# K and V rows of half the heads swapped by halves, scores by quadrants in one visit, intra products in two halves

## The chip, the cores and the metric

The kernel runs on one core of a Trainium2 chip. The metric is the device time of one execution, in microseconds (us); smaller is better. Before the change it is 224.65 us, the median of 8 runs (224.59 to 225.79).

## What is computed

The reference is a linear attention with decay over 4 batch rows, 8 heads, 768 positions and head dimension 64, followed by a gated layer on all 3072 tokens:

```python
for b in range(nb):
    ...
    intra = np.einsum('bhic,bhjc->bhij', qb, kb) * Dmask[None]
    intra = np.einsum('bhij,bhjd->bhid', intra, vb)
    inter = np.einsum('bhid,bhde->bhie', qb * lam_pow[None], kv_state)
    out[:, :, sl] = intra + inter
    ...
    kv_state = lam_block[None, :, None, None] * kv_state + np.einsum('bhsd,bhse->bhde', kb_dec, vb)
...
gate = 1.0 / (1.0 + np.exp(-(x @ w_gate)))
val = x @ w_val
return (gate * val @ w_out).astype(np.float32)
```

`Dmask` is zero where a key comes after its query (`rel < 0`), and `lam` to the power of their distance elsewhere. The result does not depend on the block length: the reference uses 64 positions, the kernel 128.

## The kernel before, in words

The 768 positions are 6 blocks (`NSTEP`) of 128 (`C`), numbered 0 to 5. One block holds 4 images (batch rows, `B`) of 8 heads, so 512 tokens. For each block the kernel runs attention and then the gated layer: `gv` computes the 12 hidden tiles (for each, four matmuls with WG, L432, a sigmoid on ScalarE, L435, four matmuls with WV, L438, a product on VectorE, L441), and `piece_po` the 12 matmuls of one output tile of 128 tokens (L495), its copy (L498) and its store (L503). The order of the work on every engine is written out by hand: each engine executes its instructions in the order of the program, and the attention of block n+1 is written in between the gated layer of block n (lines 691 to 722).

In blocks 2 to 5, which the change touches, the attention has these steps.

- **Loads** (`load`, L70): GpSimd issues DMAs that read q, k and v from HBM as float32 and write bf16. q and k are split by even and odd heads into two DMAs each (L77); v is one DMA (L91). They are issued one block ahead, behind `fade` (L394) and `make_kd` (L385), which also run on GpSimd.
- **Transposes** (`transpose_by_dma`, L229): two DMAs issued by SyncE turn q and k into QR and KR, with 64 head dimensions of two heads on the 128 partitions. `u` is the half of the partitions that a head lies on. `scale` (L242, VectorE) multiplies QR by the powers of lam and gives QS.
- **Scores** (`piece_s`, L299): for each image and head, keys by queries, 128 x 128, over 64 dimensions. `most_scores` takes images 0 to 2, with a weight tile of 64 rows and 128 columns; two heads, one on each half of the rows, run beside each other. `last_scores` takes image 3 in `parts=2`, as pieces of 64 keys, four beside each other. One PSUM bank (`sp`) holds four heads of one image. Of the four 64 x 64 quadrants of a head's scores, the one with late keys and early queries is masked to zero afterwards.
- **Masks** (`piece_m`, L204): VectorE multiplies a bank by the mask and writes bf16, 8 banks in a block.
- **Inter** (`piece_x`, L326): state Sb by QS, 32 matmuls of 64 x 64 weights and 128 queries, into four banks `op`.
- **Intra** (`add_intra` and `piece_a`, both through `intra`, L312): V of a head (128 keys by 64) by its masked scores, 128 queries, added into the same `op`; 32 in a block, two beside each other.
- **take_xt** (L343): ScalarE copies `op` to XT, the input of the gated layer. **c** (L416): the update of the state from kd and V, 32 matmuls of 64 columns, and its sum into Sb on VectorE (L423); block 5 has none.

The scores of images 0 to 2 stand between `gv(n, 10)` and `gv(n, 11)`, and the rest (`visit`) between the second and third `piece_po`. In block 5 `last_scores` stands there, and `piece_a` behind the third. Block 2 has its attention between the output tiles of blocks 0 and 1 (lines 678 to 690). PSUM has 8 banks: 5 in the pool `ps` and 3 in the pool `ff`, through which the gated layer rotates.

Of the kernel before, what the change touches and what calls it, by code (L numbers as in the profile page):

```python
# [15 lines left out]
def kernel(  # L16
# [14 lines left out]
    C = 128  # L31
# [35 lines left out]

    Q, K, V = {}, {}, {}

    def load(n, what, b0, b1):  # L70
        sl = slice(n * C, (n + 1) * C)
        for c in what:
            lst, src = {"q": (Q, q), "k": (K, k), "v": (V, v)}[c]
            if n > 1 and c != "v":
                lst[n] = qkv.tile([128, 2, B, HP, D], BF16, tag=c + "b", name=c + "b")
                for e in range(2):
                    nc.gpsimd.dma_start(  # L77
                        out=lst[n][:, e].rearrange("p b y d -> p (b y) d"),
                        in_=src[:, e::2, sl, :].rearrange("b y s d -> s (b y) d"))
# [11 lines left out]
            nc.gpsimd.dma_start(  # L91
                out=lst[n][:, b0:b1],
                in_=src[b0:b1, :, sl, :].rearrange("b h s d -> s (b h) d"))
# [77 lines left out]
    for u in range(2):  # L171
        us = slice(u * 64, (u + 1) * 64)
        nc.scalar.activation(dec[us, :].rearrange("p (e x) -> p e x", e=2),
                             lnl[us, :].rearrange("p (x u e) -> p u e x", u=2, e=2)[:, u],
                             AF.Exp, scale=float(C))
    lamq = const.tile([128, HP, C], BF16, tag="lamq")
    mask = const.tile([128, H, C], FP32, tag="mask")

    lp = const.tile([128, HP, C], FP32, tag="lp")

    def lamq_start():
        for u in range(2):
# [9 lines left out]
    def lamq_end():  # L192
        nc.vector.tensor_copy(lamq, lp)
# [6 lines left out]
    def masked(out, x, n, u):  # L200
        if n == 0:
# [6 lines left out]
    def half(e):  # L208
        return slice(e * 64, (e + 1) * 64)

    def head(g, u):
        return 4 * (g % 2) + 2 * u + g // 2
# [76 lines left out]
    def piece_s(n, bs, homes=("ps", "ps"), parts=1):  # L289
        w = C // parts  # L290
        for b in bs:
            bp, i = b // 2, b % 2
            sp = [psum_at(homes[u]) for u in range(2)]
            for hp in range(HP):
                for u in range(2):
                    us = slice(u * 64, (u + 1) * 64)
                    for z in range(parts):
                        zs = slice(z * w, (z + 1) * w)
                        nc.tensor.matmul(sp[u][zs, hp, :], lhsT=KS[n, bp][us, hp // 2, i, hp % 2, zs],  # L299
                                         rhs=QS[n, bp][us, hp // 2, i, hp % 2, :],  # L300
                                         start=(hp == 0), stop=(hp == HP - 1), skip_group_check=True)
            SP[n, b] = sp

    def piece_m(n, b, us=(0, 1)):
        if (n, b) not in MT:
            MT[n, b] = mtp.tile([128, 2, HP, C], BF16, tag="MT", name="MT")
        for u in us:
            masked(MT[n, b][:, u], SP[n, b][u], n, u)

    def intra(n, b, out, m, start, stop):  # L310
        for e in range(2):
            nc.tensor.matmul(out[half(e)], lhsT=V[n][:, b, 2 * m + e, :],  # L312
                             rhs=MT[n, b][:, e, m, :] if n == 0 else MT[n, b][:, m % 2, 2 * e + m // 2, :],
                             start=start, stop=stop, skip_group_check=True)
# [3 lines left out]
    def piece_x(n, bp, homes=("ps", "ps")):  # L318
# [3 lines left out]
        for i in range(2):  # L322
            for x in range(2):
                for u in range(2):
                    for e in range(2):
# [6 lines left out]
    def add_intra(n, b, first=True):  # L332
        bp, i = b // 2, b % 2
        for u in range(2):
            for x in range(2):
                intra(n, b, OP[bp, u][:, x, i, :], 2 * x + u, False, not first and x == 1)
# [36 lines left out]
    def make_kd(n):  # L373
        if n == 1:
            KD[n] = kdp.tile([128, 2, B * H * D // 2], BF16, tag="kd", name="kd")
            for bp in range(NB2):
                ko, ki = (x[n][:, bp].rearrange("p (e b y d) -> p e b y d", e=2, b=2, y=HP) for x in (KD, K))
                for e in range(2):
                    nc.gpsimd.tensor_tensor(
                        out=ko[:, e], in0=ki[:, e],  # L380
                        in1=kds[:, e::2].unsqueeze(1).unsqueeze(3).to_broadcast([128, 2, HP, D]), op=ALU.mult)
            return
        KD[n] = kdp.tile([128, 2, B, HP, D], BF16, tag="kd", name="kd")
        for e in range(2):
            nc.gpsimd.tensor_tensor(  # L385
                out=KD[n][:, e], in0=K[n][:, e],
                in1=kds[:, e::2].unsqueeze(1).unsqueeze(3).to_broadcast([128, B, HP, D]), op=ALU.mult)

    SD = {}

# [119 lines left out]

    idle(10)
    nc.vector.tensor_copy(Q[0][:, 0], q01[0])
    piece_tq0([0])
    make_mask(0)
    make_mask(1)
# [46 lines left out]
    def t(n, bp):  # L562
        piece_t(n, bp)

    def most_scores(n):
        piece_s(n, [0, 1])
        piece_s(n, [2], ("ps", "ff"))
        piece_m(n, 2, (1,))

    def other_masks(n):  # L570
        piece_m(n, 0)
        piece_m(n, 1)
        piece_m(n, 2, (0,))

    def last_scores(n):
        piece_s(n, [3], parts=2)
        piece_m(n, 3)
        piece_x(n, 0)
        piece_x(n, 1, ("ps", "ff"))

    def visit(n):
        last_scores(n)
        for i in range(2):
            add_intra(n, i, i == 0)
        take_xt(n, 0)
        add_intra(n, 2)
        c(n, 0, 1, homes=("ps", "ff"))
        add_intra(n, 3, False)
        take_xt(n, 1)

    def pair(bp):
        piece_s(1, [2 * bp], ("ff", "ps"), parts=2)
# [43 lines left out]
        load_wo(i, NFT // 3)  # L636
    gv(0, 6)
    lamq_end()
    gv(0, 7)
    gv(0, 8)  # L640
    g9 = psum()
# [33 lines left out]
    make_kd(2)  # L675
    load(3, "qkv", 0, B)
    gvh(1, 1, *range(NFT))
    piece_po(0, 0)
    piece_po(0, 1)
    piece_po(0, 2)  # L680
    t(2, 0)
    t(2, 1)
    piece_po(0, 3)
    most_scores(2)
    other_masks(2)
    piece_po(1, 0)
    piece_po(1, 1)
    visit(2)
    piece_po(1, 2)
    piece_po(1, 3)  # L690
    for n in range(2, NSTEP):
        nx = n + 1
        if nx == NSTEP:
            gv(n, *range(NFT))
            for tt in range(B - 1):
                piece_po(n, tt)
            piece_last(n, B - 1)
            break
        transpose_by_dma(nx)
        gv(n, 0, 1)  # L700
        if nx + 1 < NSTEP:
            fade()
            make_kd(nx)
            load(nx + 1, "qkv", 0, B)
        gv(n, 2, 3, 4, 5, 6, 7, 8)
        t(nx, 0)
        gv(n, 9)
        t(nx, 1)
        gv(n, 10)
        most_scores(nx)  # L710
        gv(n, 11)
        other_masks(nx)
        piece_po(n, 0)
        piece_po(n, 1)
# [38 lines left out]
```

## Time and profile before

| | |
|---|---|
| time, median of 8 runs | 224.65 us |
| the profiled execution, its time | 224.72 us |
| its span, first to last instruction | 222.9 us |
| granted TensorE clock | 1.00 |
| L204, a mask of one bank (128x512) on VectorE | 683 ns, 40 in blocks 1 to 5 |
| L242, the scaling of half a block's QR | 685 ns |
| L77, issue of a DMA of q or k on GpSimd | 1183 and 1178 ns |
| L385, half of kd on GpSimd | 1908 ns |
| L343, copy of one bank to XT on ScalarE | 599 ns |

The profile is one execution. Its busy times are per engine; a wait is charged to what released it. The weight load of a matmul is a row of its own (PEld). The duration of a matmul in these rows, some 200 to 400 ns, is its whole passage through the array; matmuls overlap, so what one costs is the distance of its start from the next start. Tile sizes in front of a matmul's shape, such as 64*128, are the rows and columns of the array that it uses.

### The profile page before, as it was taken

To read this page: it belongs to the slowest core of one execution; us is meant where nothing else is said; L and a number is where in the kernel's file an instruction comes from. 1 tells how busy PE (TensorE), PEld (TensorE's weight loads), DVE (VectorE), ACT (ScalarE), POOL (GpSimd) and SP (SyncE) were. 2 spreads that over 40 slices of the span, in tenths; PEclk is the share of its full clock that TensorE was granted. 3 is DMA by queue.
4 is the path that set the end of the run, shared out by engine and by line. 5 is a ranking of instruction groups with operands and counts; after the bars stand their busy time and mean duration, and the time that the engine had idled before them with its cause. 6 is when DMAs were issued, how large, how long until landed. Compare 5 with 4: busy or idle time off the path is not lost.

```text
span 222.9 us, 4362 instructions
## 1 busy us (share of the span) xinstructions
PE 214.9 (96%) x1786; PEld 114.2 (51%) x1808; DVE 106.6 (48%) x193; ACT 79.3 (36%) x151; POOL 79.2 (36%) x78
## 2 busy tenths in 40 slices
PE   7689999999999999999999999999999999999994
PEld 2444455888854564444464444564444445444443
DVE  7797658596412641346740435760335750333300
ACT  5664333435412243333243333152333225333221
POOL 8997698993593049700029900000000000000000
PEclk9999999999999999999999999999999999999999
DMA  6999999999999992999722999721900021100022
GB/s 109 156 168 193 192 176 156 156 195 172 157 141 177 241 218 100 120 151 156 48 97 85 129 149 156 48 97 49 235 0 0 3 93 51 47 0 0 3 94 96
DMA packets 106420, 25.72 MB, mean 115 GB/s; under 512 B 97056, under 2 KB 103456, under 8 KB 106400
## 3 DMA queue, kind: packets, MB, share of 16 engines
q0 software_dynamic: 81792, 13.90, 82.3%
q1 hardware_dynamic: 23568, 11.28, 23.8%
q10 hardware_dynamic: 1040, 0.26, 0.5%
q8 instruction: 14, 0.23, 0.4%
q14 instruction: 6, 0.05, 0.1%
HBM read 28.32 MB, written 6.29 MB: 155 GB/s over the span
## 4 chain that ended last, share of the span: by engine, by line
PE 92%; DMA 3%; POOL 3%; issue 1%; ACT 0%; DVE 0%; POOLq 0%
PE po L495 27%; PE vp L438 20%; PE gp L432 20%; PE gp L446 6%; PE gp L467 5%; PE vp L473 5%; DMA vb<-in_v_dram 3%; PE op L312 3%; PE sp L299 3%; PE po L484 1%; POOL kb L91 1%; PE cp L416 1%; PE op L326 1%; POOL qb L91 1%; POOL vb L91 1%
## 5 line engine op out<-in xcount | busy, mean ns | idle before, releaser
L441 DVE TENSOR_TENSOR ht<-sg,vp 128x512 bf16<-128x512 bf16 x52 | 35.7, 687 | 70.4 <-PE vp L438 69.3
L495 PE MATMUL po<-WO,ht 128*128 128x512 bf16 x266 | 60.9, 379 | 0.6
L438 PE MATMUL vp<-XT,WV 128*128 128x512 bf16 x203 | 52.9, 379 | 0.4
L432 PE MATMUL gp<-XT,WG 128*128 128x512 bf16 x204 | 52.5, 379 | 0.2 <-issue 0.2
L435 ACT ACTIVATE sg<-gp 128x512 bf16<-128x512 f32 x52 | 31.0, 597 | 59.9 <-PE gp L432 56.5
L495 PEld LDWEIGHTS <-ht 128*128 128x128 bf16 x276 | 26.5, 98 | 31.5
L438 PEld LDWEIGHTS <-WV 128*128 128x128 bf16 x208 | 20.3, 98 | 24.6
L432 PEld LDWEIGHTS <-WG 128*128 128x128 bf16 x208 | 20.0, 98 | 24.0
L498 ACT COPY ob<-po 128x512 f32<-128x512 f32 x23 | 13.5, 586 | 50.3 <-PE po L495 48.5
L204 DVE TENSOR_TENSOR MT<-sp,mask 128x512 bf16<-128x512 f32 x40 | 25.2, 683 | 11.3 <-PE sp L299 11.3
L394 POOL TENSOR_TENSOR sd<-Sb,dec 128x512 f32<-128x512 bf16 x8 | 8.1, 1038 | 35.5 <-DVE Sb L423 35.4
L467 PE MATMUL gp<-XT,WG 128*128 128x256 bf16 x96 | 14.4, 273 | 0.0
L473 PE MATMUL vp<-XT,WV 128*128 128x256 bf16 x96 | 14.4, 273 | 0.0
L477 DVE TENSOR_TENSOR ht<-sg,vp 128x256 bf16<-128x256 bf16 x24 | 10.0, 420 | 8.4 <-PE vp L473 8.4
L470 ACT ACTIVATE sg<-gp 128x256 bf16<-128x256 f32 x24 | 9.2, 385 | 12.7 <-PE gp L467 12.7
L91 POOL DMA_DIRECT2D vb<-in_v_dram x10 | 12.7, 1278 | 2.4 <-issue 1.8
L385 POOL TENSOR_TENSOR kd<-kb,kds 128x1024 bf16<-128x1024 bf16 x6 | 11.3, 1908 | 5.0 <-PE gp L467 5.0
L343 ACT CAST XT<-op 128x512 bf16<-128x512 f32 x19 | 9.9, 599 | 2.4 <-PE op L312 2.4
L473 PEld LDWEIGHTS <-WV 128*128 128x128 bf16 x96 | 9.4, 98 | 1.1
L467 PEld LDWEIGHTS <-WG 128*128 128x128 bf16 x96 | 9.2, 98 | 1.4
L77 POOL DMA_DIRECT2D qb<-in_q_dram x8 | 9.4, 1183 | 0.0
L77 POOL DMA_DIRECT2D kb<-in_k_dram x8 | 9.3, 1178 | 0.0
(82 smaller groups left out, 165.4 us busy)
## 6 DMA issues: line engine op xcount, KB each, us to landing
out_dram<-ob SPq DMA_DIRECT2D x21, 256.0 KB, 2.0
kb<-in_k_dram POOLq DMA_DIRECT2D x10, 256.0 KB, 12.8
qb<-in_q_dram POOLq DMA_DIRECT2D x8, 256.0 KB, 10.1
vb<-in_v_dram POOLq DMA_DIRECT2D x4, 512.0 KB, 16.5
WO<-in_moe_w_out_dram POOLq DMA_DIRECT2D x3, 512.0 KB, 8.1
WV<-in_moe_w_val_dram POOLq DMA_DIRECT2D x5, 256.0 KB, 8.9
WG<-in_moe_w_gate_dram POOLq DMA_DIRECT2D x4, 256.0 KB, 8.5
qb<-in_q_dram POOLq DMA_DIRECT2D x6, 128.0 KB, 8.5
```

The costliest lines, as they stand in the source:

```text
L77: nc.gpsimd.dma_start(out=lst[n][:, e].rearrange("p b y d -> p (b y) d"), in_=src[:, e::2, sl, :].rearrange("b y s d -> s (b y) d"))
L91: nc.gpsimd.dma_start(out=lst[n][:, b0:b1], in_=src[b0:b1, :, sl, :].rearrange("b h s d -> s (b h) d"))
L204: nc.vector.tensor_tensor(out=out.rearrange("p (e x) c -> p e x c", e=2), in0=x.rearrange("p (e x) c -> p e x c", e=2), in1=mask.rearrange ...
L432: nc.tensor.matmul(gp, lhsT=WG[:, mt, fs], rhs=x[:, mt, :], start=(mt == 0), stop=(mt == NMT - 1))
L435: nc.scalar.activation(sg, gp, AF.Sigmoid)
L438: nc.tensor.matmul(vp, lhsT=WV[:, mt, fs], rhs=x[:, mt, :], start=(mt == 0), stop=(mt == NMT - 1))
L441: nc.vector.tensor_mul(HT[n, ft], sg, vp)
L446: nc.tensor.matmul(ps[:, lo:hi], lhsT=W[:, mt, ft * 128:(ft + 1) * 128], rhs=x[:, mt, lo:hi], start=(mt == 0), stop=(mt == NMT - 1))
L467: nc.tensor.matmul(gp[:, cs], lhsT=WG[:, mt, fs], rhs=x[:, mt, cs], start=(mt == 0), stop=(mt == NMT - 1))
L473: nc.tensor.matmul(vp[:, cs], lhsT=WV[:, mt, fs], rhs=x[:, mt, cs], start=(mt == 0), stop=(mt == NMT - 1))
L495: nc.tensor.matmul(po, lhsT=HT[n, ft][:, tt * 128:(tt + 1) * 128], rhs=WO[:, ft, :], start=(ft == 0), stop=(ft == NFT - 1))
L498: nc.scalar.copy(ob, po)
```

## The change

K and V of blocks 2 to 5 are loaded so that heads 1, 2, 5 and 6 have their two halves of 64 rows (positions) swapped: `turned` issues, for K and for V, two DMAs for heads in order and four for the swapped ones, each on 64 partitions. Tables for swapped rows are made once (`other_halves`, `half_tables`, `make_mask3`), and `make_kd` uses such a table. The scores of all four images are computed in one visit (`all_scores`), 64 keys at a time: where keys are the early half, against all 128 queries, and where they are the late half, against the late 64 queries only. The remaining three quadrants of a head are packed into 6 banks instead of 8 (`slot`), and 6 masks take the place of 8. The intra product is done in two halves: for early queries over 64 keys (`intra_low`), for late queries over 128 keys (`intra_high`). A drain of TensorE stands between the inter products and `intra_low`. In block 2 the scores and the visit each stand one output tile later than before; in blocks 3 to 5 all scores stand where `most_scores` stood, and in block 5 the whole visit where `last_scores` stood.

```diff
+    def turned(src, n, dst):
+        for r in (0, 3, 1, 2):
+            halves = [(slice(0, 128), 0, C)] if r in (0, 3) else [(half(z), (1 - z) * 64, 64) for z in range(2)]
+            for rows, lo, k in halves:
+                nc.gpsimd.dma_start(
+                    out=dst(rows, r).rearrange("p b y d -> p (b y) d"),
+                    in_=src[:, r::4, n * C + lo:n * C + lo + k, :].rearrange("b y s d -> s (b y) d"))
...
-            if n > 1 and c != "v":
+            if n > 1 and c == "k":
+                lst[n] = qkv.tile([128, 2, B, HP, D], BF16, tag=c + "b", name=c + "b")
+                turned(src, n, lambda rows, r: lst[n][rows, r % 2, :, r // 2::2, :])
+                continue
+            if n > 1 and c == "v":
+                lst[n] = qkv.tile([128, B, H, D], BF16, tag=c + "b", name=c + "b")
+                turned(src, n, lambda rows, r: lst[n][rows, :, r::4, :])
+                continue
+            if n > 1:
...
+    def other_halves():
+        for z, d in ((0, -64.0), (1, 64.0)):
+            nc.vector.tensor_scalar_add(jns[half(z)], jn[half(z)], d)
+        for t, i in ((pks, 0), (kd4, 1)):
+            nc.scalar.activation(t, lnl, AF.Exp, scale=jns[:, i:i + 1])
+
+    def half_tables():
+        for z, d in ((0, 64.0), (1, -64.0)):
+            nc.vector.tensor_scalar_add(p1s[half(z)], p1[half(z)], d)
+        nc.vector.tensor_scalar(out=tris, in0=ip1, scalar1=p1s, scalar2=None, op0=ALU.is_ge)
+        nc.vector.tensor_copy(kds2, kds)
+        nc.vector.tensor_copy(kds2.rearrange("p (x r) -> p x r", r=4)[:, :, 1:3],
+                              kd4.rearrange("p (x r) -> p x r", r=4)[:, :, 1:3])
...
+    def make_mask3():
+        m3 = mask3.rearrange("p u t (s c) -> p u t s c", c=64)
+        def put(out, rows, cols, u, e):
...
+            nc.vector.tensor_tensor(
+                out=out, in0=t[rows, cols].unsqueeze(1).unsqueeze(1).to_broadcast([k, 3, 2, 64]),
+                in1=p[rows, 2 * u + e::4].unsqueeze(1).unsqueeze(3).to_broadcast([k, 3, 2, 64]), op=ALU.mult)
+        for u in range(2):
+            for e in range(2):
+                put(m3[:, u, :, 1 + e:5 + e:3, :], slice(0, 128), slice(64, 128), u, e)
+            for z in range(2):
+                put(m3[half(z), u, :, 0:4:3, :], half(z), slice(0, 64), u, u ^ z)
+        for t, f in ((0, slice(0, 2)), (1, slice(2, 6, 3)), (2, slice(3, 5))):
+            nc.vector.tensor_copy(m3[:, :, t, 6:8, :], m3[:, :, 0, f, :])
...
-    lp = const.tile([128, HP, C], FP32, tag="lp")
+    lp = mask3[:, 0, 0, :].rearrange("p (h c) -> p h c", h=HP)
...
+    def slot(b, x, k):
+        return (b, 3 * x + k) if b < 3 else (1, 6 + x) if k == 2 else (2 * x, 6 + k)
...
+    def all_scores(n):
+        for t in range(3):
+            for u in range(2):
+                ST[t, u] = granules(psum_at("ff" if t == 2 and u else "ps").rearrange("p h c -> p (h c)"))
+            MU[n, t] = mtp.tile([128, 2, TCH], BF16, tag="MT", name="MT")
+        for b in range(B):
+            bp, i = b // 2, b % 2
+            for x in range(2):
+                for low in (True, False):
+                    for e in range(2):
+                        for u in range(2):
+                            z = half(u ^ e if low else 1 - (u ^ e))
+                            w = KS[n, bp][half(u), e, i, x, z]
+                            r = QS[n, bp][half(u), e, i, x, :].rearrange("p (k c) -> p k c", c=64)
+                            (t, s0), (t1, s1) = slot(b, x, 0), slot(b, x, 1 + e)
+                            if low and t == t1:
+                                nc.tensor.matmul(ST[t, u][z, s0:s1 + 1:s1 - s0, :], lhsT=w, rhs=r,
+                                                 start=(b < 3 and x == 0), stop=False, skip_group_check=True)
+                                continue
+                            if low:
+                                nc.tensor.matmul(ST[t, u][z, s0, :], lhsT=w, rhs=r[:, 0, :],
+                                                 start=False, stop=False, skip_group_check=True)
+                            nc.tensor.matmul(ST[t1, u][z, s1, :], lhsT=w, rhs=r[:, 1, :],
+                                             start=False, stop=False, skip_group_check=True)
+
+    def all_masks(n, *which):
+        for t, u in which:
+            nc.vector.tensor_tensor(out=granules(MU[n, t][:, u, :]), in0=ST[t, u],
+                                    in1=granules(mask3[:, u, t, :]), op=ALU.mult)
+
+    def intra_low(n, b, x, e):
...
+        for u in range(2):
+            rows = half(u ^ e)
+            nc.tensor.matmul(OP[bp, u][half(e), x, i, 0:64], lhsT=V[n][rows, b, 4 * x + 2 * u + e, :],
+                             rhs=MU[n, t][rows, u, s0 * 64:(s0 + 1) * 64], ...
+
+    def intra_high(n, b):
...
+        for u in range(2):
+            for x in range(2):
+                for e in range(2):
+                    t, s0 = slot(b, x, 1 + e)
+                    nc.tensor.matmul(OP[bp, u][half(e), x, i, 64:128],
+                                     lhsT=V[n][:, b, 4 * x + 2 * u + e, :],
+                                     rhs=MU[n, t][:, u, s0 * 64:(s0 + 1) * 64], ...
...
-                in1=kds[:, e::2].unsqueeze(1).unsqueeze(3).to_broadcast([128, B, HP, D]), op=ALU.mult)
+                in1=kds2[:, e::2].unsqueeze(1).unsqueeze(3).to_broadcast([128, B, HP, D]), op=ALU.mult)
...
     def visit(n):
-        last_scores(n)
-        for i in range(2):
-            add_intra(n, i, i == 0)
-        take_xt(n, 0)
-        add_intra(n, 2)
-        c(n, 0, 1, homes=("ps", "ff"))
-        add_intra(n, 3, False)
-        take_xt(n, 1)
+        for bp in range(NB2):
+            piece_x(n, bp)
+        nc.tensor.drain()
+        for e in range(2):
+            for i in range(2):
+                for x in range(2):
+                    intra_low(n, i, x, 1 - e)
+                    intra_low(n, 2 + i, x, e)
+        for bp in range(NB2):
+            for i in range(2):
+                intra_high(n, 2 * bp + i)
+            take_xt(n, bp)
+        if n + 1 < NSTEP:
+            c(n, 0, 1, homes=("ps", "ff"))
...
     piece_po(0, 3)
-    most_scores(2)
-    other_masks(2)
     piece_po(1, 0)
+    all_scores(2)
+    all_masks(2, (2, 1), (0, 0), (0, 1), (1, 0), (1, 1), (2, 0))
     piece_po(1, 1)
+    piece_po(1, 2)
     visit(2)
-    piece_po(1, 2)
     piece_po(1, 3)
...
-        most_scores(nx)
+        all_scores(nx)
+        all_masks(nx, (2, 1))
         gv(n, 11)
-        other_masks(nx)
+        all_masks(nx, (0, 0), (0, 1), (1, 0), (1, 1), (2, 0))
         piece_po(n, 0)
         piece_po(n, 1)
-        if nx + 1 < NSTEP:
-            visit(nx)
-            piece_po(n, 2)
-        else:
-            last_scores(nx)
-            piece_po(n, 2)
-            piece_a(nx, 0, 1)
+        visit(nx)
+        piece_po(n, 2)
         piece_po(n, 3)
```

Left out of the diff are the declarations of the new tables and the places of three calls: `other_halves()` behind the copy of q at L512, `half_tables()` behind `lamq_end()` at L638, and `make_mask3()` in front of `piece_po(0, 0)` at L678.

More of the change, by code (lines that the diff above doesn't have):

```diff
@@ L68, with half @@
     Q, K, V = {}, {}, {}
+    def half(e):
+        return slice(e * 64, (e + 1) * 64)
+    def turned(src, n, dst):
[5 more added lines that the diff above has]
+                    in_=src[:, r::4, n * C + lo:n * C + lo + k, :].rearrange("b y s d -> s (b y) d"))
     def load(n, what, b0, b1):
@@ L175, with granules @@
                              AF.Exp, scale=float(C))
+    jns = const.tile([128, 2], FP32, tag="jns")
+    pks = const.tile([128, H], FP32, tag="pks")
+    kd4 = const.tile([128, H], FP32, tag="kd4")
+    kds2 = const.tile([128, H], FP32, tag="kds2")
+    tris = const.tile([128, C], FP32, tag="tris")
+    p1s = const.tile([128, 1], FP32, tag="p1s")
+    mask3 = const.tile([128, 2, 3, TCH], FP32, tag="mask3")
+    def other_halves():
[10 more added lines that the diff above has]
+                              kd4.rearrange("p (x r) -> p x r", r=4)[:, :, 1:3])
+    def granules(t):
+        return t.rearrange("p (s c) -> p s c", c=64)
+    def make_mask3():
+        m3 = mask3.rearrange("p u t (s c) -> p u t s c", c=64)
+        def put(out, rows, cols, u, e):
+            t, p = (tris, pks) if u ^ e else (tri, pk)
+            k = rows.stop - rows.start
+            nc.vector.tensor_tensor(
[8 more added lines that the diff above has]
+            nc.vector.tensor_copy(m3[:, :, t, 6:8, :], m3[:, :, 0, f, :])
     lamq = const.tile([128, HP, C], BF16, tag="lamq")
     mask = const.tile([128, H, C], FP32, tag="mask")
-    lp = const.tile([128, HP, C], FP32, tag="lp")
+    lp = mask3[:, 0, 0, :].rearrange("p (h c) -> p h c", h=HP)
     def lamq_start():
@@ L206, in masked @@
             in1=mask.rearrange("p (x u e) c -> p u e x c", u=2, e=2)[:, u], op=ALU.mult)
-    def half(e):
-        return slice(e * 64, (e + 1) * 64)
     def head(g, u):
@@ L302, in piece_s @@
             SP[n, b] = sp
+    def slot(b, x, k):
+        return (b, 3 * x + k) if b < 3 else (1, 6 + x) if k == 2 else (2 * x, 6 + k)
+    ST, MU = {}, {}
+    def all_scores(n):
[22 more added lines that the diff above has]
+                                             start=False, stop=False, skip_group_check=True)
@@ new lines, in all_masks @@
+    def all_masks(n, *which):
[3 more added lines that the diff above has]
+    def intra_low(n, b, x, e):
+        bp, i = b // 2, b % 2
+        t, s0 = slot(b, x, 0)
+        for u in range(2):
+            rows = half(u ^ e)
+            nc.tensor.matmul(OP[bp, u][half(e), x, i, 0:64], lhsT=V[n][rows, b, 4 * x + 2 * u + e, :],
+                             rhs=MU[n, t][rows, u, s0 * 64:(s0 + 1) * 64],
+                             start=False, stop=False, skip_group_check=True)
@@ new lines, in intra_high @@
+    def intra_high(n, b):
+        bp, i = b // 2, b % 2
+        for u in range(2):
[4 more added lines that the diff above has]
+                                     lhsT=V[n][:, b, 4 * x + 2 * u + e, :],
+                                     rhs=MU[n, t][:, u, s0 * 64:(s0 + 1) * 64],
+                                     start=False, stop=False, skip_group_check=True)
@@ L330, in piece_x @@
                                          skip_group_check=True)
[L332 to L336, printed above, removed]
     def take_xt(n, bp):
@@ L512 @@
     nc.vector.tensor_copy(Q[0][:, 0], q01[0])
+    other_halves()
     piece_tq0([0])
@@ L563, in t @@
         piece_t(n, bp)
[L565 to L579, printed above, removed]
-    def visit(n):
-        last_scores(n)
-        for i in range(2):
-            add_intra(n, i, i == 0)
-        take_xt(n, 0)
-        add_intra(n, 2)
-        c(n, 0, 1, homes=("ps", "ff"))
-        add_intra(n, 3, False)
-        take_xt(n, 1)
+    def visit(n):
+        for bp in range(NB2):
[12 more added lines that the diff above has]
+            c(n, 0, 1, homes=("ps", "ff"))
     def pair(bp):
@@ L638 @@
     lamq_end()
+    half_tables()
     gv(0, 7)
@@ L677 @@
     gvh(1, 1, *range(NFT))
+    make_mask3()
     piece_po(0, 0)
```

## Prediction

> **What bounds the kernel.** I read the page first, by engine and by chain.
>
> ```profile
> PE 214.9 (96%) x1786; PEld 114.2 (51%) x1808; DVE 106.6 (48%) x193; ACT 79.3 (36%) x151; POOL 79.2 (36%) x78
> PE 92%; DMA 3%; POOL 3%; issue 1%; ACT 0%; DVE 0%; POOLq 0%
> ```
>
> TensorE carries 92% of the chain. The remaining 8% lies at the start: in the chain's list in order of time, loads end at 13.4 us, and from 19.3 us on it names TensorE alone. From there every nanosecond added to TensorE's order moves the end, and work on another engine moves it only if TensorE comes to wait. So I read TensorE's timeline around the attention of block 3:
>
> ```profile
> 105.13 0.84 PE L299 MATMUL sp<-QS,KR 64*128 64x128 bf16 x24
> 105.91 1.04 PE L432 MATMUL gp<-XT,WG 128*128 128x512 bf16 x4
> 106.78 1.03 PE L438 MATMUL vp<-XT,WV 128*128 128x512 bf16 x4
> ...
> 112.39 0.59 PE L495 MATMUL po<-WO,ht 128*128 128x512 bf16 x2
> 112.92 0.42 PE L299 MATMUL sp<-QS,KR 64*64 64x128 bf16 x16
> 113.17 0.62 PE L326 MATMUL op<-QS,Sb 64*64 64x128 bf16 x32
> 113.71 0.86 PE L312 MATMUL op<-MT,vb 128*64 128x128 bf16 x24
> 114.41 0.67 PE L416 MATMUL cp<-vb,kd 128*64 128x64 bf16 x32
> 114.91 0.39 PE L312 MATMUL op<-MT,vb 128*64 128x128 bf16 x8
> 115.24 1.04 PE L495 MATMUL po<-WO,ht 128*128 128x512 bf16 x3
> ```
>
> The first column is the start, and the distance of two starts is the price. A matmul of 512 columns costs 0.216 (four in 0.87 from L432 to L438), so the one before the scores is over at 105.04 and the output tile at 112.82. The single records under these rows show how tiles share the array: matmuls on different parts start 3 ns apart, and then nothing starts until 56 ns after the first. Such a step holds two matmuls of 64*128 or 128*64, or four of 64*64, with 128 queries. L416, with 64 columns, has steps of 31.7 ns (16 in 0.50) for two. A change of the tile form adds 0.09 to 0.10 each time.
>
> The attention of block 3 then costs 105.91 - 105.04 = 0.87 for `most_scores` and 115.24 - 112.82 = 2.42 for the visit. Blocks 2 and 4 have the same. Block 5 has 0.87, then 0.89 (scores of image 3 and inter) and 1.11 (`piece_a`, two more form changes), by the starts at 181.69 to 182.48 and 185.18 to 186.19.
>
> **The change on TensorE, part by part.**
>
> *Scores.* 24 + 16 matmuls become 68 on 64*64: per image and pair of heads on a half (`x`), four early-key ones and four late-key ones; in image 3 the early ones are partly cut in two, so 48 + 20. Two bounds. From below, the parts of the array: in the order written, the two early matmuls of e=0 and the two late ones of e=1 use the same parts, and likewise the other two, so a late pair waits for an early one: 56 + 32 + some 14 of order = 102 ns per group. Six groups are 0.61; the two groups of image 3, with one more 64-column step and its order, 0.14 each: 0.89. From above, the pace of the matmuls: no stretch of the trace sustains one (with its weight load) in less than 14 ns (56/4 in L326), and L416, which streams half as much, needs 15.9. At that pace 68 cost 0.95 to 1.08. I take 0.98, near the 64*64 row. With form changes (0.095 + 0.014 in, 0.094 out) 1.18 in place of 0.87: **+0.31**. The dead quadrant gives little back, because what is left comes in more pieces.
>
> *Visit.* The four score steps and one form stay or go as follows. Form change in 0.11; inter 8 steps x 56 = 0.45; drain; `intra_low` 32 matmuls of 64*64 with 64 queries; form change 0.10; `intra_high` 32 of exactly L416's form and size, 16 x 31.7 = 0.51; c 0.51; form change out 0.10.
>
> The drain has no row. From below it is what a form change costs, 0.10; from above the last matmul's whole passage (216 ns, of which 160 are not its own step) and a restart, for which L299 starts 0.1 behind the copy that it waits for at 8.53 us, make 0.26, and a refill of the queue behind it as much as 0.15 more. I take 0.25. `intra_low`: from below 8 steps of 31.7 = 0.25, from above 14 ns each = 0.45; I take 0.35, between. Together 0.11 + 0.45 + 0.25 + 0.35 + 0.10 + 0.51 + 0.51 + 0.10 = 2.38 against 2.42: **-0.04**.
>
> Per block 2 to 4: +0.27. Block 5 has no c: 1.87 against 0.89 + 1.11 = 2.00, one pair of form changes saved; -0.13 + 0.31 = +0.18. Sum: 3 x 0.27 + 0.18 = **+0.99**.
>
> Here the Trainium skill speaks against the change. "TensorE: Matmul & The Clock Gate", section "Back-to-back issue gap", has the distance of starts not fall under some 25 ns however few the columns; "TensorEngine Tiling (Array Packing)", "Instruction Overhead", puts some 60 cycles on every matmul and warns against tiling a dimension that is small already. The rows disagree for matmuls on different parts: 3 ns apart, 14 on average. By the rule 68 scores cost 1.7 and `intra_low` 0.8, some 1.2 more in each block, 4.7 in all. The measured rows decide; the rule is a rival below.
>
> **What moves beside TensorE.** *Masks:* 8 x 683 ns become 6; VectorE waits for TensorE already, so this gives nothing. The last mask must be ready for `intra_low`: in blocks 3 to 5 five masks (3.4) follow `ht` of tile 11 and end near 112.3, the visit starts at 113.1. In block 2 six masks (4.1) start at the scores' end, and two output tiles (5.2) lie ahead of the visit: 1.1 spare.
>
> *Tables:* two VectorE operations of 0.15 after the copy of q fall into its 0.57 idle before QS; two ScalarE ones of 0.29 end at 7.75, before the copy of KS at 7.99. `half_tables`, some 0.9, overruns VectorE's idle 0.70 at 29.2 by 0.18, and TensorE needs that product's bank only at 31.5. `make_mask3` is 8 x 0.55 (between 424 ns for 256 columns and 682 for 512) + 3 x 0.42 = 5.7, in VectorE's 5.4 idle while it waits for QR; QS comes at most 0.5 later, and the scores of block 2 move from 72.5 to 75.1 by the output tile put ahead. Without that cover 0.5 would be lost once.
>
> *Loads.* They are the part with real distance from a cheap answer.
>
> ```profile
> 45.75 2.33 POOL L77 DMA_DIRECT2D kb<-in_k_dram  x2
> 48.01 1.74 POOL L91 DMA_DIRECT2D vb<-in_v_dram  x1
> ...
> 58.40 3.78 POOL L385 TENSOR_TENSOR kd<-kb,kds 128x1024 bf16<-128x1024 bf16 x2 [5.00 <-PE gp L467]
> ...
> 61.66 5.77 SPq L229 DMA_TRANSPOSE KR<-kb  x1
> ```
>
> Bytes and row pieces stay the same; issues go from 5 to 14 per block. An issue of a quarter takes 0.88 (L85, the same shape), of an eighth about 0.76 (L97, as many rows): K 4.8 in place of 2.3, V 4.8 in place of 1.7, +5.5 of GpSimd per block. In the compiled order each issue also waits for the landing of the eighth issue before it. Behind that wait stand `fade`, `make_kd` and the next load on GpSimd; behind a late KR on SyncE stand the stores of block 0, whose four buffers ScalarE's copies need. For block 2: K's last pieces are issued behind the landing of WO (near 51.5), so K lands about when it does now (58.4), before SyncE reaches KR (61.7). V's last pieces wait for K's, are issued near 60, and need 6.2 to 16.5 (loads of 128 and 512 KB) to land: 66 to 77, wanted at about 82. `make_kd(2)` and load 3 slip some 3 to 5 us; load 3's K is wanted at 91.5 and issued from 66. In later blocks GpSimd is idle 22.4 ahead of `fade` and has the room. I cost all this at nothing; without that cover each us late is a us on TensorE.
>
> The sum: 224.72 of the profiled execution + 0.99 = 225.7; the median lies 0.07 lower, so **225.6**.
>
> **Rivals.**
>
> *The pace is set by the parts of the array alone.* For it: the 3 ns starts, and weight loads that start right behind the matmul whose part they refill. Against: L416's 15.9. Scores 0.89 (+0.23), `intra_low` 0.25, drain 0.10: visit 2.13 (-0.29), so -0.06 per block and -0.15 in block 5: -0.33, **224.3**, not slower. It decides from a drain under about 0.16 with `intra_low` at 0.25. Did the late scores hide wholly between the early ones (56 + 32 per group), 0.2 more per block would go: 223.5.
>
> *The queue of matmuls starves* at 25 ns each as the rule says: +5.7 by the sums above, **230.3**. Against it stands every step of four.
>
> *K or V of block 2 late*, by some 1.5 beyond its margin, through the waits for the eighth issue: 225.6 + 1.5 = **227.1**. For: the load queue is busy throughout 40 to 83 us. Against: margins of 5 us.
>
> **Chances and range.** 0.3% (0.67 us) is about what a measurement of this kernel can tell from no change. The forecast has 0.52 (0.44 slower, 0.08 within; its own range 225.1 to 226.6), parts alone 0.32 (0.12 faster, 0.20 within), late loads 0.11, starving 0.05. Faster 0.12, within 0.28, slower 0.60. The range 224.1 to 227.1 leaves out the best of the parts' case and the starved one.
>
> **What would show it.** Starts between the last `gv(n, 10)` matmul and `gv(n, 11)`: 1.18 right, 1.10 parts alone, over 1.5 starved. The hole between L326's last step and the first `intra_low`: 0.25 or 0.10. `intra_high` steps of 31.7. In block 2, a hole ahead of scores or of `intra_low` charged to a DMA of KR or V would be the late loads. I am wrong if the starts in `intra_low` step by 32 ns and the drain is no longer than a form change.

## The result and the profile after

| | before | after |
|---|---|---|
| time, median | 224.63 us (54 runs) | 225.27 us (19 runs) |
| ratio, 95% interval | 1 | 1.0033 [1.0023, 1.0042] |
| the profiled execution, its time | 224.72 us | 225.44 us |
| its span | 222.9 us | 223.7 us |
| first output tile's first matmul to the last matmul | 157.83 us | 157.68 us |

The kernel became 0.64 us slower. Some runs of most kernels here, of before too, lie about 1 us above the rest; nothing below rests on them unless it says so.

The last row of the table holds the surprise. It spans all that the prediction priced on TensorE, the attention of blocks 2 to 5, and it became 0.15 us shorter. The loss lies ahead of it, in the start, to which the prediction gave nothing.

The page of the kernel after, by engine and by chain:

```profile
PE 214.7 (96%) x2026; PEld 115.3 (52%) x2048; DVE 112.8 (50%) x203; ACT 79.7 (36%) x153; POOL 99.2 (44%) x114
...
PEclk9799999999999999999999999999999999999999
...
PE 92%; DMA 3%; ACT 2%; issue 1%; DVE 0%; POOLq 0%
```

240 matmuls more, and TensorE is busy as long as before. New is the 7 in the clock row, in the second slice of 5.6 us.

TensorE's timeline around the attention of block 3, after the change (first column the start, second the length):

```profile
105.04 1.03 PE L546 MATMUL vp<-XT,WV 128*128 128x512 bf16 x4
106.00 0.25 PE L384 MATMUL sp<-QS,KR 64*64 64x128 bf16 x4
106.08 0.20 PE L390 MATMUL sp<-QS,KR 64*64 64x64 bf16 x4
106.10 0.23 PE L384 MATMUL sp<-QS,KR 64*64 64x128 bf16 x4
106.16 0.20 PE L390 MATMUL sp<-QS,KR 64*64 64x64 bf16 x4
106.19 0.23 PE L384 MATMUL sp<-QS,KR 64*64 64x128 bf16 x4
...
106.83 0.39 PE L540 MATMUL gp<-XT,WG 128*128 128x512 bf16 x1
...
113.84 0.64 PE L440 MATMUL op<-QS,Sb 64*64 64x128 bf16 x32
114.58 0.45 PE L403 MATMUL op<-MT,vb 64*64 64x64 bf16 x32
114.96 0.70 PE L413 MATMUL op<-MT,vb 128*64 128x64 bf16 x32
115.48 0.67 PE L524 MATMUL cp<-vb,kd 128*64 128x64 bf16 x32
116.09 0.82 PE L603 MATMUL po<-WO,ht 128*128 128x512 bf16 x2
```

From one L384 row to the next are 0.09 us: that is a group of four early-key and four late-key matmuls. By the single records the last matmul of `gv(n, 10)` started at 105.686 and that of the output tile ahead of the visit at 113.536. So the scores cost 106.834 - 105.902 = 0.93 (before 0.87), and the visit 116.091 - 113.752 = 2.34 (before 2.41). The attention of block 3 costs what it cost.

The loss shows in the chain of waits in order of time. Before:

```profile
5.51 1.72 POOL vb L91 x2
7.23 6.19 DMA vb<-in_v_dram
```

After:

```profile
1.25 6.78 DMA kb<-in_k_dram
8.02 0.05 issue
8.07 1.01 PE tk L297 x8
9.08 0.43 PE wm L172
```

These loads belong to blocks 0 and 1, whose code the change does not touch. Yet the first K load, issued at 1.26 and 1.25, lands at 8.02 instead of 7.51, and the last of the first V loads at 14.26 instead of 13.42. On TensorE, before:

```profile
7.56 0.62 PE L238 MATMUL tk<-ident,kb 128*128 128x128 bf16 x8 [0.45 <-DMA kb<-in_k_dram]
...
17.04 1.03 PE L446 MATMUL gp<-XT,WG 128*128 128x512 bf16 x3
```

and after:

```profile
8.07 1.01 PE L297 MATMUL tk<-ident,kb 128*128 128x128 bf16 x8 [0.78 <-DMA kb<-in_k_dram]
...
17.92 0.38 PE L554 MATMUL gp<-XT,WG 128*128 128x512 bf16 x1
```

TensorE waits 0.78 instead of 0.45 for K, and is 0.88 late at its first wide tile. It stays that late: the first output tile starts at 62.02 before and at 62.90 after. 0.87 of start less 0.15 of attention is the 0.72 between the two profiled executions. Between the medians the start has 0.64 + 0.15 = 0.79.

The loads ask for the same bytes in the same order. What each took is in the stretch from 8 to 14 us (columns: the stretch and its length; busy time and instructions of PE, PEld, DVE, ACT, POOL; granted clock; mean busy share of the DMA engines, which goes above 1 because packets overlap on an engine; GB/s). Before:

```profile
8.00:14.00 6.00, 4.50 (x77) 2.70 (x73) 5.20 (x11) 4.77 (x8) 5.78 (x9) 1.00 2.30 160
```

After:

```profile
8.00:14.00 6.00, 5.27 (x69) 3.96 (x71) 4.39 (x10) 3.57 (x6) 4.95 (x8) 0.72 3.08 151
```

The DMA engines are charged a third more time (3.08 against 2.30) and move less. A packet here is mostly one row of 128 bytes, the 64 dimensions of one head and position in bf16. By the packets' records such a row took 32.0 ns before and 42.2 on average after, from 8 to 11 us.

The clock of 0.72 is half speed from 8.1 to 11.6 us. TensorE has no gap there (busy 3.41 of 3.41 us) and is slower: the eight transposes of K in the chain above take 1.01 instead of 0.62. The ten runs of the kernel after with a mean clock of 1.0 took 225.22 to 225.27, some 0.2 less than the profiled one at 225.44. So I estimate the clock's part in the profile at 0.2, and it is not what makes the median.

### The profile page after: what moved, and what is told of

Read it like the earlier page. It is cut to its first block, busy times and chain, and to the rows that moved or that the text cites. A ratio compares the mean times of both kernels' runs of the same rounds, so it can differ in the third digit from the quotient of the medians.

```text
span 223.7 us, 4894 instructions
## 1 busy us (share of the span) xinstructions
PE 214.7 (96%) x2026; PEld 115.3 (52%) x2048; DVE 112.8 (50%) x203; ACT 79.7 (36%) x153; POOL 99.2 (44%) x114
## 4 chain that ended last, share of the span: by engine, by line
PE 92%; DMA 3%; ACT 2%; issue 1%; DVE 0%; POOLq 0%
PE po L603 27%; PE vp L546 20%; PE gp L540 20%; PE gp L554 6%; PE gp L575 5%; PE vp L581 5%; DMA kb<-in_k_dram 3%; PE op L440 1%; PE po L592 1%; PE op L413 1%; PE cp L524 1%; PE sp L384 1%; PE sp L358 1%; PE tk L297 1%; PE op L403 1%
## 5 line engine op out<-in xcount | busy, mean ns | idle before, releaser
L77 POOL DMA_DIRECT2D vb<-in_v_dram x24 | 18.0, 755 | 16.8 <-DMA qb<-in_q_dram 12.7
L77 POOL DMA_DIRECT2D kb<-in_k_dram x24 | 18.1, 789 | 4.2 <-DMA WO<-in_moe_w_out_dram 4.2
L395 DVE TENSOR_TENSOR MT<-sp,mask 128x512 bf16<-128x512 f32 x24 | 15.0, 681 | 2.1 <-PE sp L390 1.9
L531 DVE TENSOR_TENSOR Sb<-cp,sd 128x512 bf16<-128x512 f32 x8 | 5.2, 686 | 10.9 <-PE cp L524 10.9
```

Of the source, the lines that this page charges most:

```text
L77: nc.gpsimd.dma_start(out=dst(rows, r).rearrange("p b y d -> p (b y) d"), in_=src[:, r::4, n * C + lo:n * C + lo + k, :].rearrange("b y s ...
L395: nc.vector.tensor_tensor(out=granules(MU[n, t][:, u, :]), in0=ST[t, u], in1=granules(mask3[:, u, t, :]), op=ALU.mult)
```

## The experiments

Two things of the change are at work in the first 17 us: the small tables of `other_halves` (VectorE and ScalarE), and, if it counts, the place of the tiles in the on-chip memory. The compiled program puts the constants (the tiles of the pool `const`) ahead of the other pools, and the new ones are 10,912 bytes a partition more. So the q, k and v tiles of all blocks move from addresses that are multiples of 128 (the first k: 84,736) to such as leave a remainder of 32 (95,648). A row of 128 bytes then lies across a multiple of 128. This was the theory; its rival was the small tables. In the tables below "address" is that remainder, "share" the DMA share from 8 to 14 us, and "array" the time from the first output tile's first matmul to the last matmul in the profile.

### Address or small tables

`e1_after_aligned` moves the tiles of the changed kernel by 32 bytes, to a remainder of 64. That would be enough if multiples of 64 were what counts:

```diff
     mask3 = const.tile([128, 2, 3, TCH], FP32, tag="mask3")
+    pad = const.tile([128, 8], FP32, tag="pad")
```

> The changed kernel with an unused tile of 32 bytes per partition behind its new tables, so that every tile of the pools (K, V, Q among them) lies at a multiple of 64 bytes again, as before; nothing else. Theory of the addresses (the tables moved the tiles by 32 modulo 64, and the loads of 128-byte rows write more slowly there, late at the start): 0.6 to 0.8 under the changed kernel, 224.4 to 224.6. Theory of the array (the prediction: pieces and drain on TensorE): no change, 225.25. Theory of the small tables (their four operations delay VectorE and ScalarE at the start): no change, 225.25.

`e2_before_shifted` puts the same unused tile ahead of `lamq` in the kernel before (remainder 32).

> The kernel before with the same unused tile of 32 bytes, which moves its tiles from multiples of 64 bytes to 32 behind them; no instruction is added. Theory of the addresses: slower by 0.6 to 0.8, near 225.3. Theory of the array and theory of the small tables: no change, 224.63.

`e3_before_small_tables` gives the kernel before the small tables, and 32 bytes that bring the remainder back to 0:

```diff
...
     nc.vector.tensor_copy(Q[0][:, 0], q01[0])
+    other_halves()
     piece_tq0([0])
```

> The kernel before with the four operations of other_halves where the change has them (two on VectorE, two on ScalarE, their results unused), tiles kept at multiples of 64 bytes. Theory of the small tables: slower by 0.5 or more. Theory of the addresses: no change, at most 0.2. Theory of the array: no change.

`e4_late_small_tables` moves that call in the changed kernel behind the first transposes, to the line ahead of the sigmoid's table load.

> The changed kernel with other_halves called later, ahead of the load of the sigmoid table, so that its operations no longer stand in front of the first QS and KS; tiles at 32 behind multiples of 64. Theory of the small tables: faster by 0.5 or more, near 224.7. Theory of the addresses and theory of the array: no change, 225.1 to 225.3.

| | address | time (runs) | ratio to before | first K lands | share |
|---|---|---|---|---|---|
| e1 | 64 | 225.30 (22) | 1.0038 [1.0025, 1.0052] | 8.04 | 3.10 |
| e2 | 32 | 227.12 (6) | 1.009 [1.0069, 1.011] | 8.51 | 3.03 |
| e3 | 0 | 225.06 (14) | 1.0005 [0.9989, 1.002] | 7.38 | 2.30 |
| e4 | 32 | 225.85 (10) | 1.0045 [1.0026, 1.0064] | 7.99 | 2.99 |

The small tables fall as the cause: alone they cost nothing that shows (e3, whose runs, 224.59 to 225.72, lie about where those of before do, 224.55 to 225.66), and taken out of the start they give nothing back (e4). e4 is even slower, by 0.2 in its three runs at full clock (225.44 to 225.47); why was not looked into. e1 moved the tiles and gained nothing, so an address theory on 64 bytes falls as well. But e2, the kernel before with 32 unused bytes and nothing else, loses 2.4 us, three times the 0.79 that the change loses at its start. It adds no instruction, so the size of the program is not the cause either.

### 128 bytes

`f1_after_at128` is the changed kernel with 96 bytes more, remainder 0; `f2_before_plus64` and `f3_before_plus160` are the kernel before with 64 and 160 unused bytes (f3 checks e2, in whose profile all loads had started late).

```diff
     mask3 = const.tile([128, 2, 3, TCH], FP32, tag="mask3")
+    pad = const.tile([128, 24], FP32, tag="pad")
```

> The changed kernel with an unused tile of 96 bytes per partition behind its new tables, so that the tiles of the pools lie at multiples of 128 bytes, as in the kernel before (in e1 they lay at 64 behind one, in the change at 32). Theory of the addresses, now modulo 128: the first K load lands near 7.5 us instead of 8.0, and the time is 224.4 to 224.6, since TensorE's stretch from the first output tile to its last matmul is 0.15 shorter than before in the traces of the change, e1 and e4. Rival, the program's size or its new instructions set the pace of the first loads: first K at 8.0 again, 225.25.

> The kernel before with an unused tile of 64 bytes: its tiles of the pools lie at 64 behind multiples of 128; no instruction is added. Addresses modulo 128: first K near 8.0, time 225.2 to 225.6. Addresses modulo 64: no change, 224.63. Size of the program: no change.

> The kernel before with an unused tile of 160 bytes: tiles at 32 behind multiples of 128, as in e2, at other addresses. Addresses: slower, 225.2 or more; near 227.1 if all of e2's loss comes from the offset, near 225.4 if its late first DMA (lam at 4.30 instead of 3.82 us) and its later loss were of that one program. Size of the program: no change, 224.63.

`f4_after_at128_whole_loads` is f1 with the loads of K and V of blocks 2 to 5 as before the change, two DMAs and one in place of six and six. It leaves out the swap of rows on which the scores and the intra product rely, and serves for the time alone:

```diff
...
-                turned(src, n, lambda rows, r: lst[n][rows, :, r::4, :])
+                nc.gpsimd.dma_start(
+                    out=lst[n],
+                    in_=src[:, :, sl, :].rearrange("b h s d -> s (b h) d"))
```

> As f1, and K and V of blocks 2 to 5 loaded as before, in two DMAs and one, with no rows swapped (the score and intra products of the middle heads then use wrong rows; the work on the engines is the same). Theory that the 14 instead of 5 loads cost nothing: the same time as f1 within 0.1. Theory that they cost something through DMA or GpSimd: faster than f1 by that.

| | address | time (runs) | ratio to before | first K lands | share | array |
|---|---|---|---|---|---|---|
| f1 | 0 | 224.47 (12) | 0.9986 [0.9971, 1.0001] | 7.32 | 2.30 | 157.68 |
| f2 | 64 | 227.15 (6) | 1.0097 [1.0075, 1.012] | 8.96 | 3.08 | 158.75 |
| f3 | 32 | 226.90 (6) | 1.0087 [1.0067, 1.0107] | 7.99 | 3.04 | 159.21 |
| f4 | 0 | 224.44 (12) | 0.9987 [0.9974, 1.0] | 7.36 | 2.29 | 157.68 |

The theory holds at 128 bytes. In the profiles of e2 and f2 the very first load, lam, already lands late (at 4.30 and 4.68 us instead of 3.81), which is part of their late K; f3, with lam at 3.82, loses 2.2 us without that. With 96 unused bytes the changed kernel wins 0.80 us, all that it had lost and 0.2 more. Its stretch from 8 to 14 us:

```profile
8.00:14.00 6.00, 4.31 (x73) 2.62 (x72) 5.54 (x12) 4.74 (x9) 5.86 (x9) 1.00 2.30 160
```

The page's row of the load queue says the same of the whole execution. f1, then the changed kernel:

```profile
q0 software_dynamic: 82368, 13.90, 81.4%
```

```profile
q0 software_dynamic: 82368, 13.90, 92.0%
```

Packets and bytes are the same to the last digit, the time is not. f4 shows that the split of the loads costs no time in all.

What is left is the array column. f3 is 1.38 us longer than before in a part where the address costs the changed kernel nothing. Its timeline names the place, the scores of block 2. Before, and in f3:

```profile
72.48 0.84 PE L299 MATMUL sp<-QS,KR 64*128 64x128 bf16 x24
```

```profile
74.51 0.84 PE L300 MATMUL sp<-QS,KR 64*128 64x128 bf16 x24 [1.31 <-DMA KR<-kb]
```

K lands later in f3 (62.38 instead of 59.92), its transpose KR too (74.47 instead of 71.93), and the kernel before had only half a microsecond to spare. The change puts these scores one output tile later. Does that hide it?

### The later place of block 2

`g1_before_at32_later_scores` is f3 with block 2's scores and visit each one output tile later, as in the change. `g3_after_early_scores` is the changed kernel with these at the places of before:

```diff
-    piece_po(1, 0)
     all_scores(2)
     all_masks(2, (2, 1), (0, 0), (0, 1), (1, 0), (1, 1), (2, 0))
+    piece_po(1, 0)
     piece_po(1, 1)
+    visit(2)
     piece_po(1, 2)
-    visit(2)
```

> The kernel before with 160 bytes more of constants (tiles at 32 modulo 128, 226.9 in f3) and block 2's scores, masks and visit one output tile later, as the change has them. If the tiles at 32 delay KR of block 2 and the early scores make TensorE wait for it (f3: 11.84 us from the first output tile to the scores, against 10.46 in the kernel before), the wait goes and the time is 225.3 to 225.8. If f3 lost its time elsewhere, it stays at 226.7 to 227.1.

> The changed kernel as it is (tiles at 32 modulo 128), but block 2's scores and visit at the places of the kernel before, one output tile earlier. If KR of block 2 is late at this address and the later place hides it: 226.2 to 226.5. If the later place hides nothing: 225.2 to 225.3.

| | time (runs) | ratio to before | array |
|---|---|---|---|
| g1 | 226.50 (6), lowest 225.41 | 1.006 [1.0038, 1.0083] | 157.83 |
| g3 | 227.20 (6) | 1.010 [1.008, 1.012] | 159.67 |

Both expectations missed in the number. In g1 the wait is gone, and the array's part is to the hundredth what it is in the kernel before. But in its profile half speed fell into a stretch in which TensorE works. Its rows of two stretches:

```profile
8.00:14.00 6.00, 4.26 (x69) 2.71 (x71) 4.89 (x10) 4.04 (x7) 5.05 (x8) 0.97 3.10 151
14.00:18.00 4.00, 3.75 (x46) 2.11 (x45) 2.44 (x4) 1.31 (x4) 3.92 (x6) 0.61 1.93 177
```

From 13.7 to 17.1 us the clock is half. The same four matmuls in f3 at full speed and then in g1:

```profile
15.04 0.81 PE L447 MATMUL gp<-XT,WG 128*128 128x384 bf16 x4 [0.35 <-ACT XT L365]
```

```profile
15.30 1.44 PE L447 MATMUL gp<-XT,WG 128*128 128x384 bf16 x4 [0.25 <-ACT XT L365]
```

The first wide tile comes at 18.82 instead of f3's 17.70, which takes back 1.12 of the 1.38. The one run at 225.41 lies where g1 was expected; its mean clock is 0.992 as in the other five, and no profile of it is kept. What decides where the half speed falls was not found.

In g3 the array loses 2.0 us, more than expected, and the wait is another one. Its timeline, VectorE and then TensorE:

```profile
74.21 1.27 DVE L301 TENSOR_TENSOR QS<-QR,lamq 128x1024 bf16<-128x1024 bf16 x2
...
75.03 0.25 PE L384 MATMUL sp<-QS,KR 64*64 64x128 bf16 x4 [1.76 <-DVE QS L301]
```

KR had landed at 70.83. TensorE waits for QS, and VectorE came to it late. Before, VectorE scaled QR at once:

```profile
68.10 1.29 DVE L242 TENSOR_TENSOR QS<-QR,lamq 128x1024 bf16<-128x1024 bf16 x2 [5.38 <-DMA QR<-qb]
```

Why it is late, the kernels f1 and f4 show, which differ in the loads alone. VectorE and GpSimd in f1:

```profile
62.50 5.27 DVE L227 TENSOR_TENSOR mask<-tri,pk 128x384 f32<-128x384 f32 x1
67.69 0.54 DVE L227 TENSOR_TENSOR mask<-tris,pks 128x384 f32<-128x384 f32 x1
...
72.16 1.27 DVE L302 TENSOR_TENSOR QS<-QR,lamq 128x1024 bf16<-128x1024 bf16 x2
...
61.56 2.06 POOL L503 TENSOR_TENSOR sd<-Sb,dec 128x512 f32<-128x512 bf16 x2
63.56 3.79 POOL L494 TENSOR_TENSOR kd<-kb,kds 128x1024 bf16<-128x1024 bf16 x2
```

and in f4:

```profile
63.56 0.55 DVE L232 TENSOR_TENSOR mask<-tri,pk 128x384 f32<-128x384 f32 x1
...
68.32 1.29 DVE L307 TENSOR_TENSOR QS<-QR,lamq 128x1024 bf16<-128x1024 bf16 x2
...
58.47 3.78 POOL L499 TENSOR_TENSOR kd<-kb,kds 128x1024 bf16<-128x1024 bf16 x2 [4.14 <-DMA kb<-in_k_dram]
```

The first operation of `make_mask3` takes 0.55 in f4 and 5.27 in f1, where GpSimd runs `fade` and `make_kd` beside it; it ends at 67.77, 0.42 after `make_kd`. In the kernel after the same pair ends at 69.41 and 68.99. In g3 it is the third operation of `make_mask3` that takes long, 5.12, and it ends 0.41 after `make_kd`. In f4 `make_kd` is over at 62.25, before `make_mask3` begins. So the twelve DMAs in place of three do cost something: they put `make_kd` behind them, into the stretch of `make_mask3`, and QS is ready at 73.43 (f1) instead of 69.61 (f4). The later place hides it: the scores of block 2 start at 74.94 in f1; in the kernel after they start at 75.94, and QS is ready at 75.07.

### Which tiles, and the best version

`g2_after_rest_at32` keeps q, k and v at remainder 0 as f1, and moves all pools behind them to 32 by an unused tile in the pool of kd. `g4_after_all_at128` puts the 96 bytes ahead of WG instead, so that the weights and the first q tiles are at 0 too:

```diff
+    padk = kdp.tile([128, 8], FP32, tag="padk", bufs=1)
...
+    padw = const.tile([128, 24], FP32, tag="padw")
     WG = const.tile([128, NMT, DFF], BF16, tag="WG")
```

> The changed kernel with the tiles that loads write (q, k, v) at 0 modulo 128 as in f1, and all pools behind them (kd, sd, QS, KS, QR, KR, XT, ht, ob, Sb) at 32. If only the loads' writes care for the address: 224.4 to 224.6, as f1. If the stores' reads or the engines' reads and writes care too: up to 225.25.

> The changed kernel with 96 bytes put ahead of the weights and of the first q tiles, so that these are at 0 modulo 128 too, and all pools with them. If the first loads and the weights gain as the K and V loads did: 224.0 to 224.4. If only the pools' tiles count: 224.4 to 224.5, as f1.

| | time (runs) | ratio to before | share |
|---|---|---|---|
| g2 | 224.52 (12) | 0.9988 [0.9971, 1.0004] | 2.30 |
| g4 | 224.45 (12) | 0.9978 [0.9965, 0.9991] | 2.31 |

Only the tiles of q, k and v count, which the loads write in rows of 128 bytes. The weights, at 32 in all other kernels, gain nothing by an address of 0. f1, f4, g2 and g4 are one time. With 96 unused bytes the change is some 0.2 us faster than before. g4's interval ends below 1, those of f1 and g2 reach over it, and all lie within the 0.3% that one would call no change.

## Why the prediction was right in the time and wrong in the reason

The time is inside the range and the sign is right, but by luck. The sum that gave it is wrong twice, and the two errors nearly cancel: +0.99 forecast on the array, -0.15 found; nothing forecast for the start, +0.79 found.

*What bounds the kernel.* Right: TensorE's chain from the start's loads on, and each late microsecond of the start is late at the end.

*Scores.* The step that failed on the array is the term "I take 0.98, near the 64*64 row". By the records the eight groups take 0.74 (first start 105.995, last group's start 106.628, the change of form from about 106.74 on). The pace of no "less than 14 ns" was read off L326, whose matmuls are all 128 columns wide, four to a step of 56, and the 15.9 off L416, whose steps of 32 hold only two. Both were taken as the price of a matmul, where it was the width that set the step. Pieces of 64 columns on four parts go at four in 32 ns, 8 ns each. The lower bound failed too: 102 ns a group, where it is 87 to 89 from the second group on, 56 + 32 with nothing lost to order, and image 3, which was to take 140 a group, takes no longer. The line under the rivals, late scores that hide wholly ("56 + 32 per group"), is what happened. The changes of form are right (0.093 in, 0.095 out). +0.31 forecast, +0.06 measured.

*Visit.* The drain, without a row before, was taken at 0.25 and costs 0.265: from the last step's end at 114.316 to 114.581. That is the 0.26 of the last passage and a restart; nothing shows of the refill of up to 0.15. `intra_low` costs 0.27 against 0.35, its lower bound and not the middle. `intra_high` 0.53 against 0.51, c 0.51. -0.04 forecast, -0.07 measured; block 5's visit 1.84 against 1.87 (the first matmul behind it is missing in the records; its place follows from the next).

So a block costs -0.01 in place of +0.27, and block 5 -0.10 in place of +0.18: -0.13 in all, where the array shows -0.15.

*Tables.* `other_halves` at nothing is right (e3). `make_mask3` at 5.7 and "QS comes at most 0.5 later" failed: from its start to the start of QS are 9.7 us in f1, and QS comes 4.0 later than in the kernel before (73.43 against 69.39). The Trainium skill has the rule ("SBUF — State Buffer", section "Who interferes with whom"): a VectorE instruction with two inputs in SBUF, the on-chip memory, contends with a GpSimd instruction that reads SBUF. f1 and f4 agree, with 5.27 against 0.55. In f1 the operation began beside `fade` and lasted until both instructions of `make_kd`, too, were over. The profile of before could not warn: its VectorE work beside `make_kd`, the `ht` of L477 with one input in PSUM, keeps its 0.42. The cover that was named, the scores' later place, held with 0.9 to spare in the kernel after; without it the array lost 2.0, not 0.5 (g3).

*Loads.* At nothing, and right for the split (f4). `make_kd(2)` slipped by 6.8 where 3 to 5 were expected, and the K tile of block 2 was complete at 61.9, 2 us later than before, not at the same time. The 58.4 that the prediction took for K's landing is the start of `make_kd`; the second of K's two DMAs landed at 59.92. The margins held both.

*What was not in the sum.* This is the second step that failed, and the one that made the kernel slower. The tables were priced as instructions only, and their place at nothing. Their 10,912 bytes moved every tile of q, k and v, and that is the whole loss: +0.80 (f1 against the kernel after). No view of the profile shows an address; it stands in the compiled program, which could have been read beforehand. What it costs no row of before shows, since all its q, k and v tiles were at remainder 0.

*Rivals.* "The parts of the array alone" were right on the scores and more so, wrong on the drain (0.265, not 0.10). A starved queue is refuted by the groups of eight in 89 ns: by the rule that the prediction cites, 25 ns from start to start, the estimate is 200. K and V of block 2 late did not come about in the change, but lies close: it is what happens to the kernel before when its tiles shift (f3).

## What to carry to other kernels

A new constant is priced in bytes as well as in instructions: compare the addresses of all tiles that loads write, before and after, and if rows are short, pad until they start at multiples of 128 again, which here cost 96 bytes a partition. When code that a change doesn't touch gets slower, look there, and test it by an unused tile in the kernel before. And before an operation of VectorE with two inputs in SBUF is put into a gap, see what GpSimd does in it.

## What the runs showed of the hardware

- Rows of 128 bytes written by the loads into tiles at remainder 32 or 64 modulo 128 cost the DMA engines about a third more from 8 to 14 us (a share of 2.99 to 3.12 against 2.29 to 2.31, over the profiles of all fourteen kernels). Multiples of 128 that are not multiples of 256 are as good as those (e3, k at 84,864); a remainder of 96 was not tried. That a row across such a boundary is written in two pieces is a guess; no view shows it.
- Four matmuls of 64*64 and 64 columns, on four parts of the array, start within 15 ns, and the next four 32 ns after the first; late pieces fill in behind the early ones of the same group.
- A drain of TensorE between two products costs 0.265 us beyond the last step, about 0.17 more than a change of form.
- The late loads come with a slower clock. Seven profiles have it at half for 3.41 us near the start, all with tiles at 32 or 64 (8.1 to 11.6 in the kernel after, 13.7 to 17.1 in g1); f3, the eighth of these, keeps full speed. Over all runs at 32 or 64, 46 of 81 have a mean clock of 0.992 or less; at 0 it is two of 147, those of the kernel before beside the experiments among them. It cost some 0.2 us in the profile of the kernel after and 1.1 in g1.
- Right before the half speed TensorE was busy for 0.34 to 0.60 of 3.41 us, and in the starts of the kernels at 0 for 0.63 or more. But g3 has a stretch of 0.49 from 73.3 us on with full speed behind it, so these runs give no rule.
